# Turning the second expert's rows one feature block a step, behind the first expert's own relu outputs

## The chip, the core and the metric

The kernel runs on one core of a Trainium2 chip. The metric is the device time of one execution in microseconds (us). The core has a matrix engine (PE, with its weight loads shown apart as PEld), a vector engine (DVE), a scalar engine (ACT), GpSimd (POOL), and a queue processor (SP) that here only issues transfers. Each engine works through its own instructions in the order in which they were written into its program; an instruction that has to wait holds everything behind it on that engine.

## What is computed

Retention attention over 4 batches of 768 tokens with 8 heads, then a mixture of 8 experts in which each of the 3072 tokens goes to one expert:

```python
state = gamma * state + k[t] v[t]^T ; y[t] = scale * q[t] state      # per batch and head
x = y as (3072, 512)
e_idx = argmax(x @ w_gate)                                           # one expert per token
for e in range(8):
    h  = maximum(x[mask_e] @ w1[e], 0.0)                             # (n_e, 512) @ (512, 1024)
    ye = h @ w2[e]                                                   # (n_e, 1024) @ (1024, 512)
    out[mask_e] = gate_w * sigmoid(x @ w_output_gate)[e] * ye
```

## The kernel before

The first part of the kernel is the attention. As it goes, it writes every token's row (already multiplied by its gate) into a table in HBM, `srt`, sorted by expert with 480 slots for each. The first expert's first 256 rows (the "head") are computed while the attention ends. The second part, which the change is in, is the mixture of experts.

It works expert by expert, in **passes** `e` = 0 to 7. A pass has a fixed number of columns (one column is one token): pass 0 has the 224 slots of the first expert that the head left over, so it is the short pass; passes 1 to 7 have 436, 416, 408, 396, 384, 376 and 364. Each pass has eight **steps**, `f` = 0 to 7, one for each block of 128 of the 1024 hidden features; the text numbers the steps through, s = 8e + f. In a step:

- `stage1(s)` runs 12 matmuls into the PSUM tile `h`: four feature blocks of 128 (`dc` = 0 to 3), for each the three products high·high, high·low, low·high of numbers that are split in two parts (weights `whi` and `wlo`, rows `xh` and `xw`). Then ACT makes `hh`, the relu rounded to the matrix engine's format, and DVE makes `hl`, what the rounding left of the relu.
- `stage2` of the step two before, `stage2(s-2)`, runs 12 matmuls that add `w2` times `hh` and `hl` into the accumulators `a`. So `hh` and `hl` of step s are wanted only when stage 1 of step s+2 is done.
- `split_weights(s+6)` makes the weights of a later step: two casts on ACT (`whi`) and two subtractions on DVE (`wlo`). It waits until stage 2 of step s-2 has let go of the buffer (there are eight), and SP loads the next raw weights (`raw`, two buffers of two steps each) when both halves of a buffer have been split.
- `prep_x(e+1, dc)` turns one feature block of the next pass's rows: DVE transposes it in 32 by 32 blocks (`xt`), ACT casts it to the high part (`xh`), DVE subtracts to get the low part (`xw`). The first of the four calls also has DVE take the row numbers (`idi`) out of the loaded rows (`xl`).

The order on PE and POOL is that in which the code is written. The order on DVE and ACT in this part is chosen by the program's scheduler: it knows the data dependences, and by its own estimate of when each instruction could start it may put an instruction that is written later ahead of one that is written earlier.

The rows of pass 1 are loaded ahead of the loop, and `prep_x(1, dc)` is written in steps 4 to 7 of pass 0:

```python
if f >= 4 and e + 1 < E:
    prep_x(e + 1, f - 4)
```

What sits around it in the code:

Of the kernel before, what the change touches and what calls it, by code (L numbers as in the profile page):

```python
# [10 lines left out]
F32 = mybir.dt.float32  # L11
# [5 lines left out]
ALU = mybir.AluOpType  # L17
# [15 lines left out]
def retention_moe_kernel(  # L33
# [14 lines left out]
    nc = tc.nc  # L48
    P = 128
    B, H, S, D = q.shape  # L50
    E, DM, DF = w1.shape
# [4 lines left out]
    NDC = DM // P  # L56
# [50 lines left out]
    first = cpool.tile([P, E], F32, name="first")  # L107
# [34 lines left out]
    def load_weights(s: int):  # L142

        r, f = divmod(s, NF)
        e = rank_e[r]
        raw = wpool.tile([P, 2, 2 * DM], F32, name="raw", tag="raw", bufs=2)
        w = slice(f * P, (f + 2) * P)
        r1 = raw[:, 0].rearrange("p (dc x) -> p dc x", dc=NDC)

        nc.sync.dma_start(r1[:, 0:2], w1[ds(e, 1), 0:2 * P, w].rearrange("o (dc p) f -> p (o dc) f", p=P))  # L150
        for hf in range(2):
            nc.sync.dma_start(
                r1[64 * hf:64 * hf + 64, 2:4],
                w1[ds(e, 1), 2 * P:4 * P, w].rearrange("o (dc h p) f -> h p (o dc) f", h=2, p=64)[1 - hf],
            )
        nc.sync.dma_start(raw[:, 1].rearrange("p (z d) -> p z d", z=2), w2[ds(e, 1), w, :].rearrange("o (z p) d -> p (o z) d", p=P))
        for z in range(2):
            raws[s + z] = (r1[:, :, z * P:(z + 1) * P], raw[:, 1, z * DM:(z + 1) * DM])
# [31 lines left out]
    with ExitStack() as actx:  # L190
# [570 lines left out]
        n = NCH // 2 - 1  # L761
# [57 lines left out]
    with ExitStack() as mctx:  # L819
# [6 lines left out]
        for d in range(4):  # L826
            t = ps_a.tile([P, 512], F32, name=f"a{d}")
            nc.vector.memset(t[:, CAPS[0]:], 0.0)  # L828
            accs.append(t)
        NS = E * NF  # L830
        xs, xr, hs, ots = {}, {}, {}, {}


        PASS = [(rank_e[0] * SLOTS + HEAD, SLOTS - HEAD)]
# [1 line left out]
        def load_x(e):  # L836
            r0, n = PASS[e]
            nb = math.ceil(n / 32)
            t = mp.tile([P, NB, SEG], F32, name="xl", tag="xl")
            for a in range(4):  # L840
                ld = nc.sync.dma_start(
                    t[32 * a:32 * a + 32, 0:nb],
                    srt[ds(r0, 32 * nb), a * SEG:(a + 1) * SEG].rearrange("(n i) x -> i n x", i=32))
                if e == 0:
                    for o in sent:
                        tc.add_manual_dep(ld.ins, o.name, mybir.DependencyInfo(
                            mybir.DependencyClass.Sync, mybir.DependencyReason.DATA), reason="sorted rows complete")
            xr[e] = t

        def prep_x(e, dc):  # L850
            t = xr[e]
            nb = math.ceil(PASS[e][1] / 32)
            if dc == 0:
                xs[e] = (mp.tile([P, NDC, 32 * NB], F32R, name="xh", tag="xh"),
                         mp.tile([P, NDC, 32 * NB], F32R, name="xw", tag="xw"))
                idi = mp.tile([P, NB], I32, name="idi", tag="idi", bufs=3)
                nc.vector.tensor_copy(idi[:, 0:nb], t[:, 0:nb, P])
                xs["m", e] = idi
            xh, xl = xs[e]
            tp = mp.tile([P, 32 * NB], F32, name="xt", tag="xt", bufs=2)  # L860
            w = slice(0, 32 * nb)
            nc.vector.transpose(tp[:, w].rearrange("p (n i) -> p n i", i=32), t[:, 0:nb, dc * 32:dc * 32 + 32])
            nc.scalar.copy(xh[:, dc, w], tp[:, w])
            nc.vector.tensor_sub(xl[:, dc, w], tp[:, w], xh[:, dc, w].bitcast(F32))

        def stage1(s):
            e, f = divmod(s, NF)
            hi, lo = wts[s]
            xh, xl = xs[e]
            C = PASS[e][1]  # L870
            ps = ps_h.tile([P, 512], F32, name="h", tag="h")
            n = 0
            for dc in range(NDC):
                w = slice(dc * P, dc * P + P)
                for (l, r) in ((hi, xh), (hi, xl), (lo, xh)):
                    nc.tensor.matmul(ps[:, 0:C], l[:, 0, w], r[:, dc, 0:C], start=(n == 0), stop=(n == 3 * NDC - 1))  # L876
                    n += 1
            hh = mp.tile([P, CAPS[0]], F32R, name="hh", tag="hh", bufs=3)[:, 0:C]
            hl = mp.tile([P, CAPS[0]], F32R, name="hl", tag="hl", bufs=3)[:, 0:C]
            nc.scalar.activation(hh, ps[:, 0:C], AF.Relu)  # L880
            nc.vector.scalar_tensor_tensor(out=hl, in0=ps[:, 0:C], scalar=0.0, in1=hh.bitcast(F32),  # L881
                                           op0=ALU.max, op1=ALU.subtract)
            hs[s] = (hh, hl)

        def stage2(s):
            e, f = divmod(s, NF)
            hi, lo = wts.pop(s)
            hh, hl = hs.pop(s)
            C = PASS[e][1]
            nb = math.ceil(C / 32)  # L890
            for d in range(4):
                w = slice(d * P, d * P + P)
                for n, (l, r) in enumerate(((hi, hh), (hi, hl), (lo, hh))):
                    nc.tensor.matmul(accs[d][:, 0:C], l[:, 1, w], r, start=(f == 0 and n == 0),  # L894
                                     stop=(f == NF - 1 and n == 2))
            if f == NF - 1 and e < E - 1:

                ot = mp.tile([P, NB, P], F32, name="ot", tag="ot", bufs=2)
                for d in range(4):
                    nc.vector.transpose(ot[:, 0:nb, d * 32:d * 32 + 32],  # L900
                                        accs[d][:, 0:32 * nb].rearrange("p (n i) -> p n i", i=32))
                ots[e] = ot

        def emit(e, n):
            send(out.rearrange("t (a x) -> (t a) x", a=4), xs["m", e][:, n:n + 1], ots[e][:, n], 4 * NT)

        def stage2_last(s, tb):

            e, f = divmod(s, NF)
            hi, lo = wts[s]  # L910
            hh, hl = hs[s]
            w = slice(tb * P, min(PASS[e][1], tb * P + P))
            for n, (l, r) in enumerate(((hh, hi), (hl, hi), (hh, lo))):
                nc.tensor.matmul(accs[tb][0:w.stop - w.start], l[:, w], r[:, 1], start=(f == 0 and n == 0),
                                 stop=(f == NF - 1 and n == 2))

        def emit_last(tb):
            n = min(P, CAPS[-1] - tb * P)
            orow = mp.tile([P, DM], F32, name="orow", tag="orow", bufs=NTB)

            src = accs[tb][0:n].rearrange("p (dc a j) -> p dc a j", a=4, j=32)
            dst = orow[0:n].rearrange("p (a dc j) -> p dc a j", a=4, j=32)
            nc.scalar.copy(dst[:, 0:2], src[:, 0:2])
            nc.vector.tensor_copy(dst[:, 2:4], src[:, 2:4])
            send(out, idl[0:n, tb:tb + 1], orow[0:n], NT)
# [14 lines left out]
        for dc in range(NDC):  # L940
            prep_x(0, dc)
        loaded = split = NF
        for s in range(NS + 1):
            e, f = divmod(s, NF)
            while loaded < min(NS, s + NF + 1):
                load_weights(loaded)
                loaded += 2
            if f == 2 and 0 < e < E - 1:
                load_x(e + 1)
            if s < NS:  # L950
                stage1(s)

            k = s - 2
            if 0 <= k < NS - NF:
                stage2(k)
            elif NS - NF <= k < NS - 2:
                for tb in range(NTB):
                    stage2_last(k, tb)
            elif k == NS - 2:

                odd = nc.values_load(n_odd[0:1, 0:1], min_val=0, max_val=NT + 1)
                for tb in range(NTB):
                    for z in (NS - 2, NS - 1):
                        stage2_last(z, tb)
                    emit_last(tb)
            while split < min(NS, s + NF - 1):
                split_weights(split)
                split += 1
            if e >= 1 and s < NS and f >= 1:
                for n in range(2 * f - 2, min(math.ceil(PASS[e - 1][1] / 32), 2 * f)):  # L970
                    emit(e - 1, n)
            if f >= 4 and e + 1 < E:
                prep_x(e + 1, f - 4)
            if s == NS - NF:
                idl = load_idl(E - 1)


    with tc.If(odd > 0):  # L978
        with ExitStack() as octx:
# [75 lines left out]
            for r in range(1, E):  # L1055
                nov = nc.values_load(over[0:1, r - 1:r], min_val=0, max_val=SLOTS)
                with tc.If(nov > 0):
                    e = nc.values_load(order[0:1, r - 1:r], engines=(mybir.EngineType.SP,), min_val=0, max_val=E - 1)
# [47 lines left out]
```

## Time and profile before

| | |
|---|---|
| time, three runs | 438.88, 440.03, 442.42 us, median 440.03 |
| the profiled execution | 440.45 us, of which the span from the first to the last instruction is 438.7 us |
| PE busy | 422.5 us, 96% of the span |
| DVE, ACT, POOL busy | 251.3, 191.2, 187.6 us |
| granted clock of PE, mean | 0.995 |
| steps 0 to 7 (pass 0) | 163.2 to 183.9 us of the span |

The profile is one execution: engine by engine, it says what ran from when for how long, and behind which releaser an engine had sat idle. Times within it count from the start of the span; 1.75 us of the execution lie outside the span. A row of the timeline has the start, the duration, the engine, the line in the kernel, the operation with its output and inputs, a count where several were merged, and in brackets the idle time ahead of it with what ended it. A matmul's duration is longer than the distance to the next one, because matmuls overlap; the distance between starts is what one costs.

### The profile page before, as it was taken

The page shows a single profiled execution, that of the slowest core. Times are in us where ns is not written, and L with a number is a line of the kernel's source. Part 1 is how long each engine was busy: PE and PEld are TensorE (multiplying, and loading weights), DVE is VectorE, ACT ScalarE, POOL GpSimd, SP SyncE. Part 2 cuts the span into 40 slices and gives each one's busy share as a digit, 9 for nine tenths or more (in the row PEclk, how much of TensorE's full clock was granted, in tenths as well). Part 3 has the DMA queues.
Part 4 walks back from the last instruction along what each step waited for, and adds up shares of the span by engine and source line. Part 5 has one row for each costly group of instructions (what it writes and reads, how often), then busy time and mean ns, then how long its engine had stood idle before and what let it go on. Part 6 is the DMA issues. An engine that isn't in the chain of part 4 may idle for free.

```text
span 438.7 us, 9926 instructions
## 1 busy us (share of the span) xinstructions
PE 422.5 (96%) x3574; PEld 387.7 (88%) x3576; DVE 251.3 (57%) x669; ACT 191.2 (44%) x392; POOL 187.6 (43%) x242
## 2 busy tenths in 40 slices
PE   8999999999999998999999999999999999999993
PEld 4777877777787898999999999999999999999882
DVE  1476667667685459554754565475476476476111
ACT  3445555576763225543533443454353453454011
POOL 4433186378977207033007504702821731721722
PEclk9999999999999999999999999999999999999997
DMA  9899899999942195559337544934943953960102
GB/s 203 149 241 281 224 281 279 288 264 273 272 119 89 52 205 158 194 158 216 123 97 188 181 138 149 230 106 144 243 141 109 253 169 100 243 184 2 55 13 72
DMA packets 111172, 75.52 MB, mean 172 GB/s; under 512 B 56571, under 2 KB 98559, under 8 KB 111112
## 3 DMA queue, kind: packets, MB, share of 16 engines
q1 hardware_dynamic: 105840, 62.06, 56.4%
q0 software_dynamic: 5120, 12.69, 8.7%
q8 instruction: 30, 0.49, 0.5%
q14 instruction: 30, 0.25, 0.2%
q10 hardware_dynamic: 152, 0.03, 0.0%
HBM read 59.41 MB, written 15.83 MB: 171 GB/s over the span
## 4 chain that ended last, share of the span: by engine, by line
issue 45%; POOL 14%; PE 3%; DMA 3%; DVE 0%; POOLq 0%
POOL out_dram L182 14%; PE a L623 2%; DMA out_dram<-ot,idi 1%; PE h L605 1%; DMA out_dram<-ot,idx 1%; DVE ot L635 0%; POOLq L182 0%; DVE a L828 0%; DVE tj L801 0%; DVE no L802 0%; POOLq L978 0%
## 5 line engine op out<-in xcount | busy, mean ns | idle before, releaser
L182 POOL DMA_INDIRECT out_dram<-ot,idi x84 | 88.6, 1055 | 155.8 <-DVE ot L900 132.3
L876 PE MATMUL h<-xw,whi 128*128 128x224 f32 (+7 forms) x256 | 86.0, 336 | 0.0
L876 PE MATMUL h<-xh,whi 128*128 128x224 f32 (+7 forms) x256 | 85.9, 336 | 0.0
L876 PE MATMUL h<-xh,wlo 128*128 128x224 f32 (+7 forms) x256 | 85.9, 336 | 0.0
L894 PE MATMUL a<-hh,whi 128*128 128x224 f32 (+6 forms) x224 | 75.1, 335 | 1.1 <-ACT hh L880 1.1
L894 PE MATMUL a<-hl,whi 128*128 128x224 f32 (+6 forms) x224 | 75.3, 336 | 0.3 <-DVE hl L881 0.3
L894 PE MATMUL a<-hh,wlo 128*128 128x224 f32 (+6 forms) x224 | 75.0, 335 | 0.0
L177 DVE TENSOR_TENSOR wlo<-raw,whi 128x512 fp32r<-128x512 f32 x56 | 38.3, 684 | 58.2 <-ACT whi L173 56.6
L173 ACT CAST whi<-raw 128x512 fp32r<-128x512 f32 x64 | 39.7, 621 | 69.8 <-PE a L894 68.3
L881 DVE SCALAR_TENSOR_TENSOR hl<-h,hh 128x224 fp32r<-128x224 f32 (+7 forms) x64 | 34.8, 546 | 55.2 <-ACT hh L880 55.2
L880 ACT ACTIVATE hh<-h 128x224 fp32r<-128x224 f32 (+7 forms) x64 | 30.9, 485 | 78.8 <-PE h L876 78.7
L876 PEld LDWEIGHTS h<-xh,whi 128*128 128x128 f32 x256 | 48.2, 188 | 0.8
L876 PEld LDWEIGHTS h<-xw,whi 128*128 128x128 f32 x256 | 48.2, 188 | 0.7
L876 PEld LDWEIGHTS h<-xh,wlo 128*128 128x128 f32 x256 | 48.2, 188 | 0.5
L894 PEld LDWEIGHTS a<-hh,whi 128*128 128x128 f32 x224 | 42.2, 188 | 1.7 <-ACT hh L880 1.2
L894 PEld LDWEIGHTS a<-hl,whi 128*128 128x128 f32 x224 | 42.2, 188 | 1.0 <-DVE hl L881 0.5
L894 PEld LDWEIGHTS a<-hh,wlo 128*128 128x128 f32 x224 | 42.2, 188 | 0.4
L174 ACT CAST whi<-raw 128x512 fp32r<-128x512 f32 x64 | 39.5, 617 | 0.0
L275 POOL TENSOR_TENSOR vs<-vn,gv 128x512 f32<-128x512 f32 x24 | 25.1, 1048 | 31.4 <-DMA vn<-in_v_dram 24.7
L178 DVE TENSOR_TENSOR wlo<-raw,whi 128x512 fp32r<-128x512 f32 x56 | 38.3, 683 | 0.0
L509 POOL DMA_INDIRECT srt<-row,posi x24 | 24.5, 1020 | 28.0 <-ACT kt L282 7.5
L329 DVE TENSOR_TENSOR am<-s,mask 128x512 f32<-128x512 f32 x48 | 30.9, 684 | 8.4 <-PE s L325 8.4
(164 smaller groups left out, 656.2 us busy)
## 6 DMA issues: line engine op xcount, KB each, us to landing
raw<-in_moe_w_dram SPq DMA_DIRECT2D x32, 512.0 KB, 6.2
raw<-in_moe_w_dram SPq DMA_DIRECT2D x32, 256.0 KB, 6.1
raw<-in_moe_w_dram SPq DMA_DIRECT2D x64, 128.0 KB, 3.2
kn<-in_k_dram SPq DMA_DIRECT2D x24, 256.0 KB, 5.7
qn<-in_q_dram SPq DMA_DIRECT2D x12, 512.0 KB
vn<-in_v_dram SPq DMA_DIRECT2D x24, 256.0 KB, 5.9
srt<-zrow SPq DMA_DIRECT2D x8, 325.0 KB, 5.3
xl<-srt SPq DMA_DIRECT2D x12, 211.2 KB, 5.9
```

The source lines that it names most:

```text
L173: nc.scalar.copy(cols(hi), r1)
L174: nc.scalar.copy(perm(hi), r2)
L177: eng.tensor_sub(cols(lo), r1, cols(hi).bitcast(F32))
L178: eng.tensor_sub(perm(lo), r2, perm(hi).bitcast(F32))
L182: st = nc.gpsimd.indirect_dma_start(out=dst, out_offset=bass.IndirectOffsetOnAxis(ap=idx, axis=0), in_=src, in_offset=None, bounds_check=n ...
L275: nc.gpsimd.tensor_mul(vs[i], vn.pop(i), gv[:, c, :].unsqueeze(2).broadcast_to([P, H, D]))
L329: nc.vector.tensor_tensor(out=a, in0=pss[hh], in1=mask.unsqueeze(1).broadcast_to([P, NG, P]), op=ALU.mult)
L509: st = nc.gpsimd.indirect_dma_start(out=srt, out_offset=bass.IndirectOffsetOnAxis(ap=posi, axis=0), in_=row, in_offset=None, bounds_check= ...
L876: nc.tensor.matmul(ps[:, 0:C], l[:, 0, w], r[:, dc, 0:C], start=(n == 0), stop=(n == 3 * NDC - 1))
L880: nc.scalar.activation(hh, ps[:, 0:C], AF.Relu)
L881: nc.vector.scalar_tensor_tensor(out=hl, in0=ps[:, 0:C], scalar=0.0, in1=hh.bitcast(F32), op0=ALU.max, op1=ALU.subtract)
L894: nc.tensor.matmul(accs[d][:, 0:C], l[:, 1, w], r, start=(f == 0 and n == 0), stop=(f == NF - 1 and n == 2))
```

## The change

`prep_x` for pass 1 is written two steps earlier, in steps 2 to 5 of pass 0, and each of its transposes now has to stand, on DVE, behind the `hl` that was written last, which is that of the same step. The tie is one of order alone: it puts no semaphore into the program, and no data passes. Passes 1 to 7 keep their places. The lines behind it move by four.

```diff
-        xs, xr, hs, ots = {}, {}, {}, {}
+        xs, xr, hs, ots, last = {}, {}, {}, {}, {}
...
             w = slice(0, 32 * nb)
-            nc.vector.transpose(tp[:, w].rearrange("p (n i) -> p n i", i=32), t[:, 0:nb, dc * 32:dc * 32 + 32])
+            tr = nc.vector.transpose(tp[:, w].rearrange("p (n i) -> p n i", i=32), t[:, 0:nb, dc * 32:dc * 32 + 32])
+            if e == 1:
+
+                tc.add_manual_dep(tr.ins, last["hl"].name, mybir.DependencyInfo(
+                    mybir.DependencyClass.NoSync, mybir.DependencyReason.SCHED_ONLY), reason="hidden columns first")
             nc.scalar.copy(xh[:, dc, w], tp[:, w])
...
-            nc.vector.scalar_tensor_tensor(out=hl, in0=ps[:, 0:C], scalar=0.0, in1=hh.bitcast(F32),
-                                           op0=ALU.max, op1=ALU.subtract)
+            last["hl"] = nc.vector.scalar_tensor_tensor(out=hl, in0=ps[:, 0:C], scalar=0.0, in1=hh.bitcast(F32),
+                                                        op0=ALU.max, op1=ALU.subtract).ins
...
-            if f >= 4 and e + 1 < E:
-                prep_x(e + 1, f - 4)
+            f0 = 4 if e else 2
+            if 0 <= f - f0 < NDC and e + 1 < E:
+                prep_x(e + 1, f - f0)
```

On DVE at the start of pass 0, before the change (the first `hl` is step 0's, the other two are those of steps 1 and 2; `xl` are the rows of pass 1):

```order
L881 SCALAR_TENSOR_TENSOR hl_3378<-h_3364,hh_3377 128x224
L857 CAST idi_3515<-xl_3274 128x14
L862 STREAM_TRANSPOSE xt_3517<-xl_3274 128x448
L862 STREAM_TRANSPOSE xt_3556<-xl_3274 128x448
L864 TENSOR_TENSOR xw_3514<-xt_3517,xh_3513 128x448
L864 TENSOR_TENSOR xw_3514<-xt_3556,xh_3513 128x448
L862 STREAM_TRANSPOSE xt_3600<-xl_3274 128x448
L862 STREAM_TRANSPOSE xt_3639<-xl_3274 128x448
L864 TENSOR_TENSOR xw_3514<-xt_3600,xh_3513 128x448
L864 TENSOR_TENSOR xw_3514<-xt_3639,xh_3513 128x448
L881 SCALAR_TENSOR_TENSOR hl_3395<-h_3381,hh_3394 128x224
L881 SCALAR_TENSOR_TENSOR hl_3417<-h_3403,hh_3416 128x224
```

The same place with the change, from step 0's `hl` to step 4's:

```order
L885 SCALAR_TENSOR_TENSOR hl_3378<-h_3364,hh_3377 128x224
L857 CAST idi_3440<-xl_3274 128x14
L885 SCALAR_TENSOR_TENSOR hl_3395<-h_3381,hh_3394 128x224
L885 SCALAR_TENSOR_TENSOR hl_3417<-h_3403,hh_3416 128x224
L862 STREAM_TRANSPOSE xt_3442<-xl_3274 128x448
L868 TENSOR_TENSOR xw_3439<-xt_3442,xh_3438 128x448
L177 TENSOR_TENSOR wlo_3433<-raw_3359,whi_3432 128x512
L178 TENSOR_TENSOR wlo_3433<-raw_3359,whi_3432 128x4x4x32
L885 SCALAR_TENSOR_TENSOR hl_3460<-h_3446,hh_3459 128x224
L862 STREAM_TRANSPOSE xt_3481<-xl_3274 128x448
L868 TENSOR_TENSOR xw_3439<-xt_3481,xh_3438 128x448
```

Before, all eight instructions of the turning stood between the `hl` of step 0 and that of step 1. Now the `hl` of steps 1 and 2 come first, and one transpose with its subtraction follows each `hl` of steps 2 to 5, ahead of the weight subtractions of that step.

On ACT at the same place, before the change:

```order
L880 ACTIVATE hh_3377<-h_3364 128x224
L863 CAST xh_3513<-xt_3517 128x448
L863 CAST xh_3513<-xt_3556 128x448
L863 CAST xh_3513<-xt_3600 128x448
L863 CAST xh_3513<-xt_3639 128x448
L880 ACTIVATE hh_3394<-h_3381 128x224
L880 ACTIVATE hh_3416<-h_3403 128x224
L173 CAST whi_3432<-raw_3359 128x512
L174 CAST whi_3432<-raw_3359 128x4x4x32
```

And with it:

```order
L884 ACTIVATE hh_3377<-h_3364 128x224
L884 ACTIVATE hh_3394<-h_3381 128x224
L884 ACTIVATE hh_3416<-h_3403 128x224
L867 CAST xh_3438<-xt_3442 128x448
L173 CAST whi_3432<-raw_3359 128x512
L174 CAST whi_3432<-raw_3359 128x4x4x32
L884 ACTIVATE hh_3459<-h_3446 128x224
L867 CAST xh_3438<-xt_3481 128x448
L173 CAST whi_3475<-raw_3359 128x512
```

The four casts to `xh` have left the place ahead of the `hh` of step 1, and one now stands ahead of the weight casts of each of steps 2 to 5. On PE, POOL and SP no instruction has another place; two matmuls of pass 1's first stage 1 now carry waits for the last `xh` and `xw`. Behind step 5 the order on DVE and ACT is as it was.

## The prediction

> **What bounds the kernel now.** I read the page's busy times first, then what PE waits for from the end of the attention on, then the stretches around the one wait that matters, and last what DVE and ACT did just before it.
>
> ```profile
> PE 422.5 (96%) x3574; PEld 387.7 (88%) x3576; DVE 251.3 (57%) x669; ACT 191.2 (44%) x392; POOL 187.6 (43%) x242
> ```
>
> PE is busy 96% of the span, so time is won only by making PE idle less or do less. The change leaves PE's work alone. The waits of PE from 140 us to the end:
>
> ```profile
> PE a L894 <- ACT hh L880: 1.1, 1, 1.1
> PE a L623 <- DVE h L610: 0.7, 1, 0.7
> PE a L894 <- DVE hl L881: 0.3, 1, 0.3
> PE misc L456 <- ACT misc L421: 0.2, 1, 0.2
> ```
>
> Two of the four lines are in the mixture of experts (L894 is stage 2), each a single wait: one on `hh`, one on `hl`. Everything else that PE does from pass 0 to its end runs without a gap. The timeline of PE shows where the two waits are:
>
> ```profile
> 163.19 0.26 PE L876 MATMUL h<-xh,whi 128*128 128x224 f32 x1
> ...
> 167.20 0.28 PE L894 MATMUL a<-hh,whi 128*128 128x224 f32 x1
> ...
> 168.54 0.28 PE L876 MATMUL h<-xh,whi 128*128 128x224 f32 x1
> ...
> 171.10 0.37 PE L894 MATMUL a<-hh,whi 128*128 128x224 f32 x1 [1.05 <-ACT hh L880]
> 171.81 0.37 PE L894 MATMUL a<-hl,whi 128*128 128x224 f32 x1 [0.34 <-DVE hl L881]
> ...
> 173.13 0.28 PE L876 MATMUL h<-xh,whi 128*128 128x224 f32 x1
> ...
> 174.47 0.27 PE L894 MATMUL a<-hh,whi 128*128 128x224 f32 x1
> ```
>
> Stage 1 of step 0 begins at 163.19. Stage 2 of step 0 begins at 167.20 and stage 1 of step 3 at 168.54: 12 matmuls in 1.34 us. Stage 2 of step 1 should begin 1.34 later, at 169.88; it begins at 171.10 and stops again after one matmul. Stage 1 of step 4 begins at 173.13. The busy times in that step and the one after it, with PE's busy time and count, then PEld, DVE, ACT and POOL, the granted clock, the DMA's share and GB/s:
>
> ```profile
> 168.54:173.13 4.59, 3.19 (x26) 2.83 (x25) 4.48 (x10) 2.88 (x7) 3.68 (x4) 1.00 0.25 81
> 173.13:175.81 2.68, 2.68 (x26) 2.68 (x25) 2.02 (x5) 1.50 (x3) 1.99 (x2) 1.00 0.08 24
> ```
>
> A step with a stall takes 4.59 us, the next one, with no stall, 2.68. **The stall costs 4.59 - 2.68 = 1.91 us.** That is more than the 1.05 and 0.34 us in brackets, since the brackets count only from the modelled end of the matmul before, and each restart adds its own start-up (0.37 us against 0.27). What DVE and ACT did then:
>
> ```profile
> 166.30 0.38 DVE L881 SCALAR_TENSOR_TENSOR hl<-h,hh 128x224 fp32r<-128x224 f32 x1
> 166.60 0.17 DVE L857 CAST idi<-xl 128x14 int32<-128x14 f32 x1
> 166.68 1.16 DVE L862 STREAM_TRANSPOSE xt<-xl 128x448 f32<-128x448 f32 x2
> 167.95 1.16 DVE L864 TENSOR_TENSOR xw<-xt,xh 128x448 fp32r<-128x448 f32 x2
> 169.03 1.16 DVE L862 STREAM_TRANSPOSE xt<-xl 128x448 f32<-128x448 f32 x2
> 170.29 1.16 DVE L864 TENSOR_TENSOR xw<-xt,xh 128x448 fp32r<-128x448 f32 x2
> 171.37 0.68 DVE L881 SCALAR_TENSOR_TENSOR hl<-h,hh 128x224 fp32r<-128x224 f32 x2
> 171.97 0.68 DVE L177 TENSOR_TENSOR wlo<-raw,whi 128x512 fp32r<-128x512 f32 x1
> 172.57 0.68 DVE L178 TENSOR_TENSOR wlo<-raw,whi 128x512 fp32r<-128x512 f32 x1
> ```
>
> ```profile
> 167.34 1.09 ACT L863 CAST xh<-xt 128x448 fp32r<-128x448 f32 x2 [2.27 <-DVE xt L862]
> 169.70 1.09 ACT L863 CAST xh<-xt 128x448 fp32r<-128x448 f32 x2 [1.26 <-DVE xt L862]
> 170.69 0.60 ACT L880 ACTIVATE hh<-h 128x224 fp32r<-128x224 f32 x2
> ```
>
> The `h` of step 1 was done before 167.20, but its `hh` ran at 170.69: ACT had the four `xh` casts ahead of it, and these waited for DVE's transposes. The `hl` of steps 1 and 2 waited at 171.37 behind all of it on DVE.
>
> **The change part by part.** No instruction is added or taken away on PE, ACT or DVE; the order moves on DVE and ACT alone.
>
> What it removes. The `hl` of steps 1 and 2 now stand right behind `idi`. A relu follows its matmuls like this, in a step with no stall:
>
> ```profile
> 174.68 0.36 ACT L880 ACTIVATE hh<-h 128x224 fp32r<-128x224 f32 x1 [0.32 <-PE h L876]
> 175.08 0.38 DVE L881 SCALAR_TENSOR_TENSOR hl<-h,hh 128x224 fp32r<-128x224 f32 x1
> ```
>
> Stage 1 gives way to the next matmul at 174.47, `hh` starts 0.21 later, `hl` 0.40 after that. `idi` starts at 166.60 as before and the transposes began at 166.68, so the `hl` of step 1 starts about there and is done at 167.06, 2.8 us before 169.88. So stage 2 of step 1 starts on time: minus 1.91 us.
>
> What it moves behind. Stage 1 of step 2 ends at 167.20, so `hl` of step 2 starts at 167.20 + 0.21 + 0.40 = 167.81. From there each step on DVE is a chain: `hl` (two in 0.60, so 0.30), transpose to `xh` (166.68 to 167.34, 0.66), `xh` to `xw` (167.34 to 167.95, 0.61), `xw` (two from 167.95 to 169.03, 0.54), and two `wlo` at 0.60: **3.31 us a step against PE's 2.68.** DVE falls behind by 0.63 us a step, for four steps. ACT's part hides in it: the weight casts stand between `xh` and the next `hh`, and beside `xw` and `wlo`. The `hl` of steps 3, 4, 5, 6 start at 171.12, 174.43, 177.74, 181.05 and take 0.38. Stage 2 wants them at 175.24, 177.92, 180.60 (2.68 apart from 169.88 on) and, for step 6, behind the first wide stage 1.
>
> ```profile
> 183.85 0.37 PE L876 MATMUL h<-xh,whi 128*128 128x436 f32 x1
> ...
> 186.47 0.54 ACT L880 ACTIVATE hh<-h 128x436 fp32r<-128x436 f32 x1 [1.39 <-PE h L876]
> ```
>
> That relu is step 8's. Before, its stage 1 began at 183.85 and ended at 186.47 - 0.21 = 186.26, 2.41 us. With the change stage 1 of step 8 begins at 183.85 - 1.91 = 181.94, and stage 2 of step 6 at 184.35. The margins are 3.7, 3.1, 2.5 and 2.9 us; the least is 2.5, at step 5. The last `xw` starts at 178.04 + 0.66 + 0.61 = 179.31 and is done by 179.93, 2 us before stage 1 of step 8 begins and 3.8 before its last three matmuls, which alone use that block. From step 6 on DVE has no turning to do and regains its lag (in the step from 173.13 it was busy for 2.02 us of 2.68). So moving costs nothing while PE's work covers it.
>
> [...] Here two `wlo` of 0.68 us start 0.60 apart, so the rows show an overlap of 0.08 us.
>
> Transfers. The next raw weights go out when two `wlo` pairs are done:
>
> ```profile
> 175.19 0.38 SPq L150 DMA_DIRECT2D raw<-in_moe_w_dram  x1
> ...
> 180.55 0.37 SPq L150 DMA_DIRECT2D raw<-in_moe_w_dram  x1
> ```
>
> By the chain the second and the fourth pair of `wlo` end at 174.5 and 181.1, against 175.1 and 180.5 before: one load 0.6 us earlier, one 0.6 us later. Either is split six steps (16 us or more) before its matmuls, so 0.6 us is hidden, as would be a few more. A split that waits for its transfer holds up the next `hh` and `hl` on ACT and DVE, which stage 2 wants two steps later. Output scatters on POOL keep their order and follow PE.
>
> What lies behind. PE has no wait after 171.81, so nothing there is tied to a clock of its own, and the 1.91 us should arrive at the end unshortened. The end itself follows PE:
>
> ```profile
> 431.29 0.40 PE L914 MATMUL a<-wlo,hh 128*108 128x512 f32 x1
> ...
> 432.86 1.01 POOL L182 DMA_INDIRECT out_dram<-orow,idl  x1 [0.43 <-DVE orow L924]
> ```
>
> The last output goes out 1.6 us after the last matmul starts; what is left of the span, to 438.7, follows it. That tail moves along.
>
> **The sum.** 0 for PE's work, -1.91 for the stall, 0 for the lag (2.5 us of cover), 0 for the transfers. The profiled execution took 440.45 us, 438.7 of span and 1.75 around it: it becomes 438.54. It stood 0.42 above the median of the three runs, 440.03; that becomes **438.1 us**, 0.4% less. A bound from both sides: the stall can give no more than 1.91, and nothing less than nothing unless a margin breaks.
>
> **The rivals.**
>
> *A. The gain is lost further on.* PE, 1.91 us ahead, meets something that it had not waited for, raw weights or the rows of a pass, and idles there. For it: the raw load at 180.55 now comes later while PE is earlier, a shift of 2.5 us against each other. Against it: splits six steps ahead, and PE's waits, which show none for over 250 us. It gives back 1.91 at most: 440.0.
>
> *B. DVE's lag breaks the margin, and it is slower.* The chain of transpose, cast and subtraction crosses to ACT and back in every step, where before it did two blocks at a time. If a round trip of 1.27 us (0.66 + 0.61) took twice that, `hl` of step 5 would come three times 1.27, 3.81 us, later against 2.5 of margin, and `hl` of step 6 four times, 5.08 against 2.9: PE would stand 2.16 us there in all, more than the 1.91 won. That gives 440.3, slower by 0.25. It begins to cost from 0.83 us more a step (2.5 / 3) and turns the sign from 1.21 (1.91 + 2.92, by 4). Something that could do it is POOL, which still scatters the head's rows then:
>
> ```profile
> 171.02 1.29 POOL L182 DMA_INDIRECT out_dram<-ot,idx  x1 [0.30 <-issue]
> 172.62 1.50 POOL L182 DMA_INDIRECT out_dram<-ot,idx  x1 [0.30 <-issue]
> 174.42 1.00 POOL L182 DMA_INDIRECT out_dram<-ot,idx  x1 [0.30 <-issue]
> ```
>
> If each of these held DVE for its whole length, 3.79 us, that alone is past the least margin by 1.3. But the `wlo` at 171.97 and 172.57 and the `hl` behind them ran beside these scatters in 0.68 us and started 0.60 apart, so they held nothing. [...]
>
> *C. The change doesn't do what it says.* The tie is one of order, and the program's order shows it; what could fail is that stage 2 of step 1 was late for another reason too. `whi` and `wlo` of that step were made during the attention, and `hl` of step 0 (166.30) came in time. I see none. It would give 440.0, like A.
>
> **How the numbers follow.** Forecast 0.82, A and C together 0.09, B 0.05, and 0.04 for what I don't see. The three runs before lie from 1.15 below to 2.39 above their median, so a median of the changed kernel may lie a good 1 us from 438.1 with the mechanism right. From 436.6 to 440.6 the range takes in the forecast with that scatter and A, C and B as priced. Over 1% (4.4 us, about what a measurement of this kernel tells from no change) faster would need more than twice the stall: 0.04. Over 1% slower would need about three times B's standstill (6.3 us): 0.03. Within 1%: 0.93.
>
> **What would show it.** In the profile after: no wait of PE on L898 (stage 2's line now) at the head of pass 0; the step that took 4.59 us takes 2.68; `hl` of steps 3 to 6 about 3.3 us apart and then closing up; stage 1 of step 8 begins 20.66 - 1.91 = 18.75 us after stage 1 of step 0 (163.19 to 183.85 before). Wrong would be: a wait of PE on `hl` in steps 5 to 8 (B), a new wait on `whi`, `wlo` or `xh` from pass 1 on (A), or a span that is shorter by clearly more than 2 us.

## The result and the profile after

The changed kernel takes 438.46 us in the median of 10 runs (437.65 to 439.10), the kernel before 440.84 (438.88 to 444.16, 10 runs): a ratio of **0.9944, 95% interval 0.9925 to 0.9963**. The prediction was 438.1 us; its ratio, 438.12 / 440.03 = 0.9957, lies inside the interval. Ratios leave out runs more than 1.5% above the fastest of their kernel; here that is none, but on chip 13 below it is 14 of the 29 runs of the kernel before and none of the changed kernel's 12, so its ratio there, 1.0074, is above the 1.0031 of the medians of all runs. The profiled execution took 438.08 us, 436.3 of span.

Busy times on the page, for the whole span:

```profile
PE 421.2 (97%) x3576; PEld 387.1 (89%) x3576; DVE 251.3 (58%) x669; ACT 190.8 (44%) x392; POOL 186.6 (43%) x242
```

The work is the same; PE's share rose from 96 to 97%. What PE waited for from 140 us to the end, as line waited at, releaser, us in total, times, longest:

```profile
PE a L623 <- DVE h L610: 0.7, 1, 0.7
PE misc L456 <- ACT misc L421: 0.2, 1, 0.2
```

Both stood there before; the two waits at stage 2 (on `hh` and `hl`) are gone, and no new one has come. The stretches: steps 0 to 7, step 3 by itself (4.59 us before), and from stage 1 of step 8 to just ahead of the last matmul. Columns as in the prediction: length, then PE, PEld, DVE, ACT, POOL busy with counts, granted clock, DMA share, GB/s.

```profile
162.52:181.28 18.76, 18.76 (x171) 18.76 (x169) 15.21 (x45) 9.82 (x22) 8.18 (x8) 1.00 0.61 176
167.87:170.55 2.68, 2.68 (x26) 2.68 (x25) 2.05 (x5) 1.86 (x4) 2.07 (x3) 1.00 0.53 176
181.28:428.70 247.42, 247.42 (x1345) 240.99 (x1344) 134.66 (x246) 98.34 (x184) 89.42 (x85) 1.00 0.55 148
```

The same two long stretches of the kernel before:

```profile
163.19:183.85 20.66, 19.26 (x170) 18.89 (x169) 16.25 (x47) 10.33 (x22) 8.85 (x8) 1.00 0.59 180
183.85:431.20 247.35, 247.35 (x1345) 240.97 (x1344) 133.80 (x243) 98.26 (x184) 89.59 (x85) 1.00 0.54 146
```

Read length against PE's busy time. Before, 20.66 us held 19.26 us of PE; now PE is busy in all of its 18.76. Behind step 8 PE has no gap in either. The last matmul started at 431.29 before; now it is this one:

```profile
428.72 0.40 PE L918 MATMUL a<-wlo,hh 128*108 128x512 f32 x1
```

From the start of stage 1 of step 8 to the start of the last matmul it is 247.44 us in both. So the 2.4 us by which the span is shorter (438.7 to 436.3) are 1.90 in steps 0 to 7, nothing behind them, -0.17 from the start of the last matmul to the end (7.41 before, 7.58 now), and 0.67 from stage 1 of step 0 beginning at 162.52 instead of 163.19. That last part lies ahead of the first instruction that the change moves, and varies from execution to execution (161.96 to 163.48 in the three profiles on chip 10 below).

DVE from the `hl` of step 0 on, as start, length, instruction, and in brackets the idle time ahead of it with its releaser:

```profile
165.63 0.38 DVE L885 SCALAR_TENSOR_TENSOR hl<-h,hh 128x224 fp32r<-128x224 f32 x1
165.94 0.16 DVE L857 CAST idi<-xl 128x14 int32<-128x14 f32 x1
166.01 0.38 DVE L885 SCALAR_TENSOR_TENSOR hl<-h,hh 128x224 fp32r<-128x224 f32 x1
167.12 0.39 DVE L885 SCALAR_TENSOR_TENSOR hl<-h,hh 128x224 fp32r<-128x224 f32 x1 [0.72 <-ACT hh L884]
167.43 0.63 DVE L862 STREAM_TRANSPOSE xt<-xl 128x448 f32<-128x448 f32 x1
168.70 0.62 DVE L868 TENSOR_TENSOR xw<-xt,xh 128x448 fp32r<-128x448 f32 x1 [0.63 <-ACT xh L867]
169.24 0.69 DVE L177 TENSOR_TENSOR wlo<-raw,whi 128x512 fp32r<-128x512 f32 x1
169.84 0.68 DVE L178 TENSOR_TENSOR wlo<-raw,whi 128x512 fp32r<-128x512 f32 x1
170.44 0.38 DVE L885 SCALAR_TENSOR_TENSOR hl<-h,hh 128x224 fp32r<-128x224 f32 x1
...
173.76 0.38 DVE L885 SCALAR_TENSOR_TENSOR hl<-h,hh 128x224 fp32r<-128x224 f32 x1
...
177.07 0.38 DVE L885 SCALAR_TENSOR_TENSOR hl<-h,hh 128x224 fp32r<-128x224 f32 x1
...
178.63 0.63 DVE L868 TENSOR_TENSOR xw<-xt,xh 128x448 fp32r<-128x448 f32 x1 [0.63 <-ACT xh L867]
...
180.38 0.39 DVE L885 SCALAR_TENSOR_TENSOR hl<-h,hh 128x224 fp32r<-128x224 f32 x1
181.88 0.38 DVE L885 SCALAR_TENSOR_TENSOR hl<-h,hh 128x224 fp32r<-128x224 f32 x1
```

The `hl` of step 1 now runs at 166.01, right behind `idi`. One step of the turning reads transpose 167.43, `xw` 168.70, two `wlo`, next `hl` 170.44. The `hl` of steps 3 to 6 start 3.32, 3.31 and 3.31 us apart, the next one 1.50 later: DVE falls behind PE for four steps and then catches up. On ACT the price of PE's being earlier shows:

```profile
185.88 0.62 ACT L173 CAST whi<-raw 128x512 fp32r<-128x512 f32 x1 [1.39 <-DMA raw<-in_moe_w_dram]
187.07 0.62 ACT L174 CAST whi<-raw 128x512 fp32r<-128x512 f32 x1 [0.58 <-DMA raw<-in_moe_w_dram]
```

The weight casts that ACT makes in step 8, for step 14, waited 1.97 us for their transfer, and PE never noticed.

### The profile page after: what moved, and what is told of

Read it like the earlier page. It is cut to its first block, busy times and chain, and to the rows that moved or that the text cites. A ratio compares the mean times of both kernels' runs of the same rounds, so it can differ in the third digit from the quotient of the medians.

```text
span 436.3 us, 9928 instructions
## 1 busy us (share of the span) xinstructions
PE 421.2 (97%) x3576; PEld 387.1 (89%) x3576; DVE 251.3 (58%) x669; ACT 190.8 (44%) x392; POOL 186.6 (43%) x242
## 4 chain that ended last, share of the span: by engine, by line
issue 44%; POOL 14%; DMA 4%; PE 3%; DVE 0%; POOLq 0%
POOL out_dram L182 14%; DMA out_dram<-ot,idi 3%; PE a L623 2%; PE h L605 1%; DMA out_dram<-ot,idx 1%; DVE ot L635 0%; POOLq L182 0%; DVE a L828 0%; DVE no L802 0%; DVE tj L801 0%; POOLq L983 0%
```

## The experiments

The first nine runs fell on three chips (13, 1 and 7) on which PE also stood idle with nothing in the profile holding it. Such waits are put down to "issue"; that PE ran short of instructions there is the author's reading, which no run tests. They came to 8.4 to 17.7 us in each profiled execution, counted from 140 us to its end. The kernel before took 466 to 474 us there; it was not profiled on these chips, but e1, which has its order on DVE and ACT, shows the same gaps. These runs are read by the waits in the first steps; their ratios are against the kernel before on the same chip, and sizes of under 1% are not carried over from them. The last three ran on chip 10, where PE had no such wait.

| run | edit | chip | median us | ratio to before (95%) |
|---|---|---|---|---|
| e0_after | none (changed kernel) | 13 | 467.62 | 1.0074 (1.0033 to 1.0116) |
| e1_move_alone | earlier place, no tie | 13 | 467.74 | 0.9997 (0.9928 to 1.0065) |
| e2_tie_alone | tie, place as before | 13 | 471.34 | 1.0154 (1.0076 to 1.0232) |
| e4_bunch_step1 | all four blocks behind `hl` of step 1 | 13 | 465.62 | 1.0013 (0.9963 to 1.0062) |
| e5_chain_twice | each block turned twice | 1 | 478.53 | 1.0078 (1.0043 to 1.0114) |
| e7_transpose_twice | only the transpose twice | 1 | 474.89 | 1.0024 (0.9992 to 1.0057) |
| e1_again | as e1 | 7 | 464.32 | 1.0015 (0.9966 to 1.0064) |
| e2_again | as e2 | 7 | 467.95 | 1.0100 (1.0044 to 1.0156) |
| e5_again | as e5 | 7 | 469.44 | 1.0091 (1.0036 to 1.0147) |
| b_before | none (kernel before) | 10 | 440.87 | 0.9979 (0.9962 to 0.9997) |
| e0_again | none (changed kernel) | 10 | 438.02 | 0.9932 (0.9906 to 0.9957) |
| e4_again | as e4 | 10 | 438.39 | 0.9930 (0.9904 to 0.9956) |

### The earlier place without the tie

```diff
-            if e == 1:
+            if False:      # the tie of the transpose behind the last hl
```

> Without the tie: prep_x(1) is written in steps 2 to 5, and the scheduler orders DVE and ACT freely. It puts all eight instructions of the turning between the hl of step 0 and that of step 1 again, as in the kernel before. Theory 'the order on DVE and ACT': the stall is back, steps 0 to 7 take 20.66 us, and the time is that of before within 0.3%. Rival 'the place in the code': with the earlier place alone 18.75 us and 1.9 us less.

> The earlier place without the tie, once more, in the hope of a chip on which PE is fed its instructions without gaps. Theory 'the order on DVE and ACT': waits of PE of 1.1 us on hh and 0.3 on hl in step 3, as in the kernel before; 20.66 us from stage 1 of step 0 to that of step 8. Rival 'the place in the code': none of it, 18.75 us. Where PE runs short of instructions again, the two waits tell, and the stretch doesn't.

PE's waits from 165 to 215 us in e1_again:

```profile
PE h L880 <- issue: 1.3, 2, 0.7
PE a L898 <- ACT xh L867: 1.1, 1, 1.1
PE a L898 <- DVE hl L885: 0.3, 1, 0.3
```

The stall is back at its old size, 1.1 and 0.3 us, and on chip 13 it was the same two numbers. (The first wait is put down to the last cast to `xh`, which ACT ran just ahead of the `hh`.) With the block's place alone, the order on DVE and ACT comes out as before the change: the scheduler puts a transpose that is ready ahead of an `hl` that is not. So it takes the tie to remove the stall, and the time of these two runs is that of the kernel before (0.9997 and 1.0015).

### The tie without the earlier place

```diff
-            f0 = 4 if e else 2
+            f0 = 4
```

> The tie without the earlier place: the blocks stand behind the hl of steps 4 to 7. Theory 'order, with a date': no wait in step 3, but the last xh and xw come too late for the last matmuls of stage 1 of step 8; worked out from the rows of before, xw of the last block is done 1.4 us after PE wants it. PE waits 1.4 to 1.5 us there, and the time is 0.3 to 0.5 us under before. Rival 'the tie is all': no wait of PE, 1.9 us less, as with the whole change.

> The tie without the earlier place, once more. Theory 'order, with a date': no wait of PE in step 3; a wait on the last xh and xw in stage 1 of step 8, 1.4 to 1.5 us on a chip that feeds PE without gaps (0.5 us where PE came late to step 8 for want of instructions), and 0.3 to 0.5 us under before. Rival 'the tie is all': no wait, 1.9 us under before.

With the turning in steps 4 to 7, stage 1 of step 8 waits for it. PE in e2_again:

```profile
191.07 0.46 PE L880 MATMUL h<-xh,whi 128*128 128x436 f32 x1 [1.99 <-ACT xh L867]
191.73 0.47 PE L880 MATMUL h<-xw,whi 128*128 128x436 f32 x1 [0.20 <-DVE xw L868]
```

2.2 us there, more than the 1.4 to 1.5 expected; 0.5 in the run on chip 13. PE had gaps in both (2.7 us put down to "issue" from 165 to 215 us in e2_again, 2.6 in e2_tie_alone), and why they differ so was not settled. No wait on `hh` or `hl` is left, so the stall has moved from stage 2 of step 1 to stage 1 of step 8. The gain in time that was expected, 0.3 to 0.5 us, did not come: by the medians of all runs e2 took 471.34 us against 466.19 on chip 13 and 467.95 against 465.67 on chip 7. How much of that is this wait and how much the gaps is not shown. The waits say that the two parts of the change need each other: the tie puts the turning behind the relu, the earlier place gets it done in time.

### All four blocks at once, one step later than before

```diff
-            f0 = 4 if e else 2
-            if 0 <= f - f0 < NDC and e + 1 < E:
-                prep_x(e + 1, f - f0)
+            if e == 0 and f == 1:
+                for dc in range(NDC):
+                    prep_x(1, dc)
+            if e and f >= 4 and e + 1 < E:
+                prep_x(e + 1, f - 4)
```

> All four blocks at once, behind the hl of step 1: only hl and hh of step 1 come ahead of the turning, those of step 2 come behind it. Theory 'only what is wanted first must come first': hl of step 2 is done 0.6 us before stage 2 of step 2 wants it, so PE doesn't wait, steps 0 to 7 take 18.75 us and the time is 1.9 us under before. Rival 'one block a step is what does it': PE waits on hl of step 2, and part of the 1.9 us is given back.

> All four blocks behind the hl of step 1, once more. On a chip without gaps: 18.75 us from stage 1 of step 0 to that of step 8, no wait on hh or hl, ratio 0.9957. With gaps: no wait on hh or hl either; theory 'supply' expects a ratio of 0.998 to 1.004, as in the first try; a ratio under 0.997 would say that this order is worth something where the changed kernel's is not.

Steps 0 to 7 of e4_again, the `hl` of step 2, which stands behind all eight instructions on DVE, and the first matmul that reads it:

```profile
163.48:182.24 18.76, 18.76 (x171) 18.76 (x169) 15.16 (x45) 9.96 (x22) 9.03 (x8) 1.00 0.68 194
```

```profile
171.97 0.38 DVE L885 SCALAR_TENSOR_TENSOR hl<-h,hh 128x224 fp32r<-128x224 f32 x1
```

```profile
172.97 0.28 PE L898 MATMUL a<-hl,whi 128*128 128x224 f32 x1
```

The `hl` is done at 172.35, 0.62 us ahead of its matmul, and PE does not stop: 18.76 us, as with the change. What cost 1.91 us was the `hh` and `hl` of one step, step 1, behind four blocks that had another 15 us; spreading them over four steps adds nothing on this chip (438.39 against 438.02). On chip 13 there was no wait on `hh` or `hl` either.

### A longer chain

For e5, each block is turned a second time (transpose, cast, subtraction); for e7, only the transpose is repeated. Both add work whose result is the same.

```diff
             nc.vector.tensor_sub(xl[:, dc, w], tp[:, w], xh[:, dc, w].bitcast(F32))
+            if e == 1:     # e5: the three instructions again (e7: the transpose alone, ahead of the cast)
+                nc.vector.transpose(tp[:, w].rearrange("p (n i) -> p n i", i=32), t[:, 0:nb, dc * 32:dc * 32 + 32])
+                nc.scalar.copy(xh[:, dc, w], tp[:, w])
+                nc.vector.tensor_sub(xl[:, dc, w], tp[:, w], xh[:, dc, w].bitcast(F32))
```

> The changed kernel with transpose, cast and subtraction of each block done twice, so each of the four steps is 1.81 us longer on DVE (0.54 + 0.66 + 0.61). Theory 'margins of 3.7, 3.1, 2.5 and 2.9 us': hl of steps 4, 5, 6 comes 0.5, 2.9, 4.3 us after PE wants it; PE waits on hl from step 6 on, 4.3 to 4.5 us in all, and the time is 4.4 us over the changed kernel, 2 to 2.5 us over before. Rival 'DVE has more room than that': less than 2 us of waits, and the time stays under before.

> The changed kernel with each transpose of the turning issued twice, 0.54 to 0.62 us more on DVE in each of the four steps. Theory 'margins': hl of step 5 comes 1.6 to 1.9 us later against 2.5, that of step 6 2.2 to 2.5 against 2.9; no wait of PE, time as the changed kernel. Rival 'DVE's lag already costs something': the time goes up by 0.5 us or more over the changed kernel.

> Transpose, cast and subtraction of each block twice, once more. On DVE a step of the chain took 5.30 us in the first try, 1.99 more than the changed kernel's 3.31. Theory 'margins of 3.7, 3.1, 2.5 and 2.9 us': hl of steps 4, 5, 6 comes 0.9, 3.5, 5.1 us after PE wants it, PE waits 4 to 5.5 us in all on a chip without gaps, and the time is 2 to 3.5 us over before. Rival 'DVE has more room': under 2 us of waits, and the time not above before.

PE in e5_again, the first matmuls that waited for ACT or DVE in these steps:

```profile
189.73 0.37 PE L902 MATMUL a<-hh,whi 128*128 128x224 f32 x1 [0.79 <-ACT hh L888]
190.60 0.37 PE L902 MATMUL a<-hl,whi 128*128 128x224 f32 x1 [0.50 <-DVE hl L889]
...
195.91 0.37 PE L902 MATMUL a<-hl,whi 128*128 128x224 f32 x1 [0.50 <-DVE hl L889]
```

A step of the chain took 5.30 us, 1.99 more, and PE waited for `hh`, `hl`, `ot` and `xw` for 3.0 us in all (1.7 us in e5_chain_twice), although gaps (2.6 us put down to "issue" in e5_again) and slower matmuls (12 of stage 2 in 2.56 us there, from 179.10 to 181.66, where 1.34 is usual) had made it 6 to 7 us late for step 7. That is rival B's mechanism at work; the 4 us and more that were expected were for a PE that is on time. The times are above the kernel before (1.0078 and 1.0091), but so was the changed kernel on chip 13, so they do not tell. In e7 the `hl` of three steps stand as follows:

```profile
180.47 0.38 DVE L886 SCALAR_TENSOR_TENSOR hl<-h,hh 128x224 fp32r<-128x224 f32 x1
184.47 0.38 DVE L886 SCALAR_TENSOR_TENSOR hl<-h,hh 128x224 fp32r<-128x224 f32 x1
188.46 0.38 DVE L886 SCALAR_TENSOR_TENSOR hl<-h,hh 128x224 fp32r<-128x224 f32 x1
```

4.00 and 3.99 apart, some 0.68 us more a step than with the change, and PE waited for none of them. The prediction put the point at 0.83 us more a step; 0.68 held and 1.99 did not, which brackets it. PE was late for step 7 in both (23.17 us behind the start of stage 1 of step 0 in e7, 22.42 in e5_again, where the changed kernel has 16.08), which makes the upper side strong and the lower one weak.

### The changed kernel once more, on chip 13

> The changed kernel once more, as the yardstick of this set. Theory 'one stall': the stretch from the start of stage 1 of step 0 to that of step 8 is 18.75 us (20.66 before), and the time is 1.9 us (0.43%) under the kernel before. Rival 'more than the stall': the ratio of 0.9944 (2.4 us) holds, and half a us comes from somewhere else.

PE's waits from 165 to 215 us, and two of its rows:

```profile
PE h L880 <- issue: 1.7, 3, 0.9
PE a L898 <- issue: 1.6, 2, 0.8
```

```profile
174.38 0.36 PE L898 MATMUL a<-hh,whi 128*128 128x224 f32 x1 [0.83 <-issue]
...
177.24 0.35 PE L880 MATMUL h<-xw,whi 128*128 128x224 f32 x1 [0.94 <-issue]
```

No wait on another engine, as the change has it, but five gaps in which nothing held PE that the profile shows, and steps 0 to 7 take 25.59 us, more than in e1 on the same chip (24.86) where the old stall was present. In both profiles PE ran nearly 7 us of these steps at half clock (a mean granted clock of 0.87 in the 25.59 us and of 0.86 in the 24.86). The gain is not seen in the time there: the ratio is 1.0074, and the medians of all runs are 467.62 and 466.19. A guess that the stall lets the instruction supply catch up, so that taking it away only uncovers the gaps, is argued and not shown: the gaps from 165 to 215 us were 0.6 and 1.3 us in the two runs with the stall against 2.6 to 3.3 in those of the changed order, but 0.9 in e4_bunch_step1, which has no stall either.

### Both kernels on chip 10

> The kernel before, unchanged, so that there is a profile of it from the same chip as the two that follow. Ratio 1.000 within 0.4%. In its profile the waits of PE of 1.1 us on hh and 0.3 on hl in step 3. If PE runs short of instructions here too, theory 'supply' (the stall lets instructions catch up, so that PE waits less for them behind it) expects gaps of PE for want of instructions between step 3 and step 8 of 1 us or less; rival 'chance' expects as many as in the changed kernel, 2.5 to 3.5 us.

> The changed kernel once more. On a chip without gaps: ratio 0.9957, 18.75 us from stage 1 of step 0 to that of step 8. With gaps: theory 'supply' expects 2.5 to 3.5 us of gaps in these steps, in the place of the stall, and a ratio between 1.000 and 1.008 as before; rival 'chance' a ratio of 0.996 and gaps as in the kernel before.

No wait of PE on chip 10 is put down to "issue", so these runs do not test the guess about the supply. The kernel before, profiled a second time: PE's waits at stage 2, steps 0 to 7, the rest, and the three steps behind the one with the stall (which took 4.60 us at full clock).

```profile
PE a L894 <- ACT hh L880: 1.1, 1, 1.1
...
PE a L894 <- DVE hl L881: 0.3, 1, 0.3
```

```profile
162.48:184.78 22.30, 20.90 (x171) 20.53 (x169) 16.33 (x47) 10.33 (x22) 8.84 (x8) 0.92 0.56 166
184.78:432.20 247.42, 247.42 (x1345) 241.05 (x1344) 133.86 (x243) 98.22 (x184) 88.99 (x85) 1.00 0.53 146
```

```profile
172.43:175.12 2.69, 2.69 (x16) 2.69 (x15) 1.71 (x4) 1.24 (x3) 1.98 (x2) 0.54 0.07 24
175.12:177.80 2.68, 2.68 (x22) 2.68 (x22) 0.71 (x2) 1.24 (x3) 0.00 (x0) 0.83 0.69 203
177.80:180.48 2.68, 2.68 (x26) 2.68 (x26) 1.59 (x4) 1.50 (x4) 0.00 (x0) 1.00 0.73 213
```

The same stall, but the granted clock behind it is 0.54 and 0.83 of full speed: in 2.69 us PE did 16 matmuls instead of 26. By the microsecond (PE busy, granted clock, DMA share, GB/s):

```profile
172.00:173.00 1.00, 1.00 (x10) 0.82 0.20 66
173.00:174.00 1.00, 1.00 (x7) 0.50 0.07 25
174.00:175.00 1.00, 1.00 (x7) 0.50 0.13 41
175.00:176.00 1.00, 1.00 (x6) 0.50 0.43 112
176.00:177.00 1.00, 1.00 (x11) 0.98 0.84 279
```

A mean of 0.82 is 0.36 us at half speed, and 0.98 is 0.04; with the three between them **half the clock for 3.40 us**. PE's matmuls start 0.21 us apart from 172.65 to 176.06, and 0.11 apart ahead of that and behind it. The half clock begins at 172.64, 1.5 us after PE had started again (171.10). Steps 0 to 7 took 22.30 us, 1.64 more than the 20.66 of the first profile, whose clock stayed at 1.00 behind the same stall. The changed kernel beside it (e0_again):

```profile
161.96:180.71 18.75, 18.75 (x170) 18.75 (x169) 15.20 (x45) 9.80 (x22) 8.19 (x8) 1.00 0.58 171
180.71:428.10 247.39, 247.39 (x1345) 241.06 (x1344) 134.74 (x246) 98.30 (x184) 88.91 (x85) 1.00 0.55 148
```

So in this pair of profiles the stall and the low clock behind it cost 22.30 - 18.75 = 3.55 us, nearly twice its price in the first pair. How often that happens can be told roughly from each run's mean clock, since 3.40 us at half speed take 0.004 off it (1.70 of 438). Of the 29 runs of the kernel before on chip 10, 7 had a mean of 0.991, the others 0.994 to 0.998; of the 22 runs of the changed kernel and e4 on undisturbed chips, none was below 0.994. (In the five profiles without gaps the clock also falls to half behind the last matmul, for 2.3 to 4.7 us of the span, where it costs nothing; that makes the rest of the spread there, and could hide a few more stretches, so 7 is the least.) The median of those 7 is 441.87 us, of the other 22 440.91, 0.96 apart where the two profiles gave 1.64 in these steps; of the 12 runs of e0_again and e4_again it is 438.21.

The same kernel against itself came out at 0.9979 (0.9962 to 0.9997): a ratio between two sets of runs can be off by 0.2%, 0.9 us, and its interval just miss the truth.

## Why the prediction was right, and its one mis-sized term

**The stall and its price.** As forecast: no wait of PE at stage 2's line, the step of 4.59 us takes 2.68, steps 0 to 7 take 18.76 us where 18.75 was worked out. Rival C, that the tie does nothing, fell with e1: without the tie the stall is back. That the time came within 0.4 us of 438.1 is luck in part: the kernel before, in ten runs, stood at 440.84 and not at 440.03, and the gain was 2.38 and not 1.91; of the 0.81 and the 0.47 us, 0.34 is left.

**DVE's lag.** As forecast to 0.01 us: 3.31 a step, and the first of the four `hl` at 170.44 where 171.12, less the 0.67 by which this execution was earlier, gives 170.45. The `xw` of the last block was done at 179.26, 2.0 us before stage 1 of step 8, as worked out. The margins were not only predicted but tried: e4 used one up to 0.62 us without loss, e5 broke them, so rival B is a real mechanism with the wrong price for this kernel. POOL's scatters held nothing on DVE; the `wlo` took 0.68 and 0.69 us beside them.

**The transfers and what lies behind.** The raw weights did come too late for their casts, by 1.39 and 0.58 us, the collision that rival A named; six steps of lead hid it. From step 8 to the last matmul it is 247.44 us before and after, so nothing was given back and rival A fell, in the profiles in which PE had no gaps put down to "issue". On chip 13, where the gain did not show, it is not settled.

**What was mis-sized.** The step that failed is the bound under the sum: "the stall can give no more than 1.91". That was read from one execution in which the clock stayed at 1.00. In another the same stall was followed by 3.40 us at half clock and gave 3.55. The span there fell by 3.8 us (439.8 to 436.0), which the prediction itself had named as a sign of being wrong. That the stall brings the low clock on is what 7 of 29 runs with it against none of 22 without it point to; no run varied the stall's length. In the execution that was hit the granted clock was 0.50 for 3.40 us, behind gaps of 1.06 and 0.34 us; why that one was hit and the other not was not shown.

Does that account for the medians? They differ by 2.38 us in the first comparison and by 3.39 on chip 10 (441.41, its 17 runs of the kernel before, to 438.02); 1.91 with about a quarter of the runs at 3.55 would give 2.3 in the mean. The 22 runs of the kernel before above a mean clock of 0.991 still lie 2.7 above the changed kernel, 0.8 more than 1.91. Stretches of low clock that the mean hides do not explain it: the 9 of these runs at 0.994 have a median of 440.93 us, the 4 at 0.998 one of 440.82. The rest is no larger than the 0.9 us by which the kernel came out different from itself, and no profile of such a run was taken on chip 10, so it stays open.

## What to carry to other kernels

Work that is ready early is not for that reason wanted early: a scheduler that places by readiness put four blocks with a use 15 us away ahead of a relu that TensorE needed in 3 us. Put the urgent thing first by a tie, and give the moved work a date as well, since the tie alone (e2) moved the stall to the date's end. When pricing a stall of TensorE, look at the granted clock behind it in several executions; in one of two profiles here a stall of 1.91 us was followed by another 1.64 us of loss.

## What the runs showed of the hardware

A stall of 1.4 us (1.06 and 0.34, with one matmul between) was followed in one execution by 3.40 us at a granted clock of 0.50 and in another by none. On chip 13 the clock of the changed kernel fell too, from 177.0 on, amid the gaps of up to 0.94 us shown above. There the stretch and one part of it read:

```profile
166.02:191.61 25.59, 22.34 (x170) 21.75 (x169) 15.59 (x46) 10.02 (x22) 7.88 (x8) 0.87 0.45 129
...
180.00:182.00 2.00, 2.00 (x11) 2.00 (x11) 1.52 (x4) 0.56 (x2) 0.00 (x0) 0.50 0.00 0
```

A mean of 0.87 over 25.59 us is 6.7 us at half speed, about twice 3.40. In e2_again, behind the wait of 1.99 us, the 12 matmuls of stage 2 took 2.54 us (192.25 to 194.79), and those of the next step 1.33 again (197.59 to 198.92). And chips differ in a way that the kernel does not set: on three of the chips PE had idle time that nothing in the profile explains, 8.4 to 17.7 us from 140 us to the end of an execution, in the other profiles none at all. What feeds it slowly there, if that is what it is, was not found, nor why the change brought nothing on the one such chip where it was timed.
